# Attention, FFN and experts on one core: smaller first FFN chunks, the first in plain float32, the weights divided during the second

## The chip, the cores and the metric

One NeuronCore of a Trainium2 chip runs the whole program. The metric is device time in microseconds of one execution, as the median of several runs. PE is TensorE, DVE is VectorE, ACT is ScalarE, POOL is GpSimd and SP is SyncE, which here only issues transfers. Every engine works through its own instructions strictly in the order in which they were written out.

## The reference

```python
# attention, 4 batches x 8 heads, 576 positions, 64 wide: only the 32 largest scores of a row count
scores = q @ k.T / sqrt(64)
kth = np.partition(scores, -32, axis=-1)[..., -32:-31]
attn = softmax(np.where(scores >= kth, scores, -1e9))
x = (attn @ v)                      # laid out as 2304 tokens x 512
# dense FFN
h = np.maximum(x @ w_in, 0.0)       # 512 x 2048, weights given in 64-bit floats
x = h * h @ w_out                   # 2048 x 512
# mixture of 8 experts, two for each token, chosen by noisy logits
logits = x @ w_gate + log1p(exp(x @ w_noise)) * noise
out[token] = sum over its two experts of weight * (relu(x @ w1[e]) @ w2[e])
```

## The kernel before

**Attention** runs as 80 *units*, one after another. A full unit is 128 queries of two heads: two score tiles of 128 x 576, and for each of them a *search* on DVE for the 32nd largest value of every row (lines L407 to L448, which end in one instruction of L448 for each search). A left unit holds the last 64 queries of two heads in one score tile, so it has one search. POOL and ACT then make the softmax (L464 to L466), PE transposes it (L477, L500, L501) and multiplies it by the values (L514), and DVE scales the result (L486 or L490), which closes the unit. ACT and POOL split it into a rounded part and a remainder (`finish`, L491, L492), which go into the tile `xT` of a chunk of tokens. There are 18 token tiles of 128; `LEFT_AFTER` says after which full tile of a batch its left units come.

**The FFN** takes *chunks* of token tiles; `CHUNKS` lists their sizes. Each chunk goes through `NF` = 16 steps f. A step multiplies `xT` by a weight tile `wi` (4 parts c) into `ph` (called `pf` in the profile while attention runs), squares its positive part, and multiplies that by a weight tile `wo` into one accumulator `acc` for each token tile. Every product is made of three float32r matmuls: high by high, high by low, low by high. *First products* below are the 12 matmuls of a step with `wi` (L319 to L321), *second products* the three matmuls for each token tile with `wo` (L305 to L307). The weights arrive as 64-bit floats. `convert` makes float32 of one of the 32 weight tiles, with two instructions each on ACT (L153, L157) and DVE (L155, L156) and one on POOL (L158), divides it in high and low on ACT and POOL (L161, L162) and stores both in DRAM (`wsc`, L163), from where each chunk loads them (L313, L315). The high half of the number is worked on in PSUM (tile `acc`) for the first `IN_PSUM` = 14 conversions and in SBUF (tile `ca`) afterwards.

**What sets the order.** The FFN steps lie in a list `background`. Between the pieces of a unit, `step(n)` takes pieces of FFN work from that list up to a credit of `n` us; the credit of a unit comes from `rate(i)`. A chunk enters the list when the last unit that feeds it has closed. Three conversions are emitted for each unit at a lower priority. A scheduler with a model of the engines then fixes every engine's order. After the last unit the rest of the FFN, the routing of the last tokens (`route`) and the experts follow. These lines carry it:

```python
CHUNKS = [3, 3, 3, 3, 3, 3]
RATE = 6.0
FIRST_RATE = 5.5
def rate(i):
    return (FIRST_RATE if state["chunk"] == 0 else RATE) * (weight[i] if i < NU else 1.0)
```

Of the kernel before, what the change touches and what calls it, by code (L numbers as in the profile page):

```python
# [8 lines left out]
F32 = mybir.dt.float32  # L9
# [8 lines left out]
P = 128  # L18
# [3 lines left out]
NEG = -3.0e38  # L22
CHUNKS = [3, 3, 3, 3, 3, 3]
LEFT_AFTER = [3, 2, 0, 2]
AHEAD = 2
# [3 lines left out]
IN_PSUM = 14  # L29
RATE = 6.0  # L30
FIRST_RATE = 5.5
LEFT_WEIGHT = 0.6
# [23 lines left out]
def attention_ffn_moe(ctx: ExitStack, tc: tile.TileContext, q, k, v, w_ffn, w_route, noise, w_exp, out,  # L56
# [23 lines left out]

    tag = "" if keep is not None else "x"
    wsc = [nc.dram_tensor(f"wsc{tag}{f}", (P, 2, 2, DM), F32, kind="Internal").ap() for f in range(NF)]
    xs = nc.dram_tensor(f"xs{tag}", (E * NT, ROW), F32, kind="Internal").ap()
# [60 lines left out]
    def convert(vpool, f, which):  # L144
        n = DM
        raw = vpool.tile([P, 2 * n], U32, name="raw", bufs=3 if keep is not None else 2)
        nc.sync.dma_start(raw, w_ffn[f, which])
        pair = raw.rearrange("p (j t) -> p j t", t=2)
        lo_w, hi_w = pair[:, :, 0], pair[:, :, 1]
        a = vpool.tile([P, n], U32, name="ca", bufs=2)  # L150

# [6 lines left out]
        nc.gpsimd.tensor_tensor(a, a, lo_w, op=ALU.add)  # L158
        val = a.bitcast(F32)
        sp = vpool.tile([P, 2, n], F32R, name="csp", bufs=2 if keep is not None else 1)  # L160
# [135 lines left out]
    after, mpools = [], []  # L296

    def ffn(t0, nt, xT):
# [12 lines left out]
        for f in range(NF):  # L311
            wi = fpool.tile([P, 2, DM], F32R, name="wi", bufs=2)
            nc.sync.dma_start(wi.bitcast(F32), wsc[f][:, 0])  # L313
            wo = fpool.tile([P, 2, DM], F32R, name="wo", bufs=2)
            nc.sync.dma_start(wo.bitcast(F32), wsc[f][:, 1])  # L315
            ph = after[0].tile([P, DM], F32, name="ph") if after else ps_f.tile([P, DM], F32, name="pf")
            for c in range(NC):
                sl = slice(c * P, (c + 1) * P)
                nc.tensor.matmul(ph[:, 0:n], wi[:, 0, sl], xT[:, 0, c, 0:n], start=(c == 0), stop=False)  # L319
# [7 lines left out]
            nc.scalar.activation(r[:, 0:n], r[:, 0:n], AF.Square)  # L327
            nc.scalar.activation(gt[:, 0, 0:n], r[:, 0:n], AF.Copy)  # L328
            nc.gpsimd.tensor_tensor(gt[:, 1, 0:n], r[:, 0:n], gt[:, 0, 0:n].bitcast(F32), op=ALU.subtract)  # L329
            yield True, 0.163 * nt  # L330
# [150 lines left out]

    def finish(av, rt, dst, j, off, n):
        x = apool.tile([P, P], F32, name="x", bufs=4)
# [192 lines left out]

    def pieces(nt):
        return NF * (NC * nt * 0.163 + nt * 0.65)

# [38 lines left out]
    vctx = ExitStack()  # L718
    vpool = vctx.enter_context(tc.tile_pool(name="vpool", bufs=2))

    def conversions():
# [8 lines left out]
    for b in range(B):  # L730
        for i in range(NFULL):
            for j in range(H // 2):
                units.append((b, i * P, True, j, tiles.index((b, i))))
                if i == LEFT_AFTER[b]:
                    units.append((b, NFULL * P, False, j, tiles.index((b - b % 2, None))))
    NU = len(units)
    chunks, t = [], 0
# [25 lines left out]
    def close(i):  # L763
# [4 lines left out]
        if full:  # L768
            if ch not in dsts:
                dsts[ch] = fpool.tile([P, 2, NC, CH], F32R, name="xT", bufs=2)  # L770
            finish(av, rt, dsts[ch], j, (t - t0) * P, P)
        else:
            if t not in lefts:
                lefts[t] = apool.tile([P, 2, NC, P], F32R, name="xL", bufs=1)
            finish(av, rt, lefts[t], j, (b % 2) * LEFT, LEFT)
        missing[ch] -= 1
        if not missing[ch]:
            for tt in range(t0, t0 + nt):
                if tt in lefts:
                    nc.gpsimd.tensor_copy(dsts[ch][:, :, :, (tt - t0) * P:(tt - t0 + 1) * P], lefts[tt])  # L780
            background.append([ffn(t0, nt, dsts[ch]), pieces(nt)])

    def rate(i):

        return (FIRST_RATE if state["chunk"] == 0 else RATE) * (weight[i] if i < NU else 1.0)

# [282 lines left out]
```

## Time and profile before

| | |
|---|---|
| Median of 3 runs | 1365.13 us (1363.53 to 1368.26) |
| Profiled execution | 1361.43 us, of which 1359.7 us are the span from first to last instruction |
| PE busy | 1240.0 us, 91% |
| DVE busy | 889.0 us, 65% |
| ACT busy | 862.3 us, 63% |
| POOL busy | 773.3 us, 57% |
| Mean granted TensorE clock | 0.971 of full speed |
| Moved by DMA | 261.65 MB |

A busy share is a mean over stretches that differ: attention with FFN work between its pieces up to 781 us of the span, then what is left of the FFN, and the experts from about 895 us on.

### The profile page before, as it was taken

The page shows a single profiled execution, that of the slowest core. Times are in us where ns is not written, and L with a number is a line of the kernel's source. Part 1 is how long each engine was busy: PE and PEld are TensorE (multiplying, and loading weights), DVE is VectorE, ACT ScalarE, POOL GpSimd, SP SyncE. Part 2 cuts the span into 40 slices and gives each one's busy share as a digit, 9 for nine tenths or more (in the row PEclk, how much of TensorE's full clock was granted, in tenths as well). Part 3 has the DMA queues.
Part 4 walks back from the last instruction along what each step waited for, and adds up shares of the span by engine and source line. Part 5 has one row for each costly group of instructions (what it writes and reads, how often), then busy time and mean ns, then how long its engine had stood idle before and what let it go on. Part 6 is the DMA issues. An engine that isn't in the chain of part 4 may idle for free.

```text
span 1359.7 us, 25767 instructions
## 1 busy us (share of the span) xinstructions
PE 1240.0 (91%) x7937; PEld 1083.3 (80%) x7937; DVE 889.0 (65%) x4531; ACT 862.3 (63%) x1849; POOL 773.3 (57%) x1239
## 2 busy tenths in 40 slices
PE   3666689889999999899999998999999999999997
PEld 2554478778887888688878887889999899899876
DVE  7999979898777888998698101255544444444554
ACT  6988888898788878988797443543433323333343
POOL 5869999867875757777656536233441331513232
PEclk9787699999999999999999999999999999999999
DMA  9996688734764356166415768645653443434464
GB/s 321 362 359 232 207 298 303 257 122 136 253 215 163 122 178 226 44 198 220 153 57 176 234 245 272 221 147 194 202 165 122 134 148 124 150 114 146 137 202 139
DMA packets 86387, 261.65 MB, mean 192 GB/s; under 512 B 10844, under 2 KB 10972, under 8 KB 86240
## 3 DMA queue, kind: packets, MB, share of 16 engines
q1 hardware_dynamic: 76960, 231.51, 51.6%
q0 software_dynamic: 9280, 28.40, 5.7%
q8 instruction: 65, 1.06, 0.3%
q14 instruction: 82, 0.67, 0.2%
HBM read 209.90 MB, written 52.06 MB: 193 GB/s over the span
## 4 chain that ended last, share of the span: by engine, by line
PE 67%; DVE 9%; DMA 7%; ACT 4%; POOL 3%; issue 2%; SPq 0%; POOLq 0%; DVEq 0%; ACTq 0%
PE ph L643 5%; PE ph L644 5%; PE ph L645 5%; PE acc L624 5%; PE acc L626 5%; PE acc L625 5%; PE pa L514 4%; PE acc L305 4%; PE acc L306 4%; PE acc L307 4%; PE ps L394 4%; PE pf L319 4%; PE pf L321 3%; PE pf L320 3%; PE pa L477 3%; DVE w L411 2%
## 5 line engine op out<-in xcount | busy, mean ns | idle before, releaser
L407 DVE MAX8 m<-sb 128x8 f32<-128x115 f32 (+1 forms) x720 | 190.4, 265 | 69.5 <-ACT sb L396 64.5
L465 POOL TENSOR_TENSOR sb<-sb,w 128x576 f32<-128x576 f32 x144 | 205.7, 1430 | 46.4 <-ACT w L464 44.0
L411 DVE MATCH_REPLACE8 w<-m,sb 128x115 f32<-128x115 f32 (+1 forms) x720 | 186.9, 262 | 0.0
L665 POOL DMA_INDIRECT out<-y,info x40 | 45.9, 1148 | 241.2 <-DVE y L664 223.5
L649 ACT ACTIVATE ht<-ph 128x384 fp32r<-128x384 f32 (+1 forms) x128 | 55.8, 436 | 194.5 <-PE ph L645 194.5
L394 PE MATMUL ps<-K,qt 128*128 128x288 f32 (+2 forms) x640 | 130.6, 333 | 43.5 <-ACT sb L396 22.3
L650 DVE SCALAR_TENSOR_TENSOR ht<-ph,ht 128x384 fp32r<-128x384 f32 (+1 forms) x128 | 62.6, 489 | 162.3 <-ACT ht L649 162.2
L643 PE MATMUL ph<-xe,wi 128*128 128x256 f32 (+1 forms) x512 | 159.4, 311 | 1.7 <-ACT wi L636 1.2
L645 PE MATMUL ph<-xe,wi 128*128 128x256 f32 (+1 forms) x512 | 158.6, 310 | 0.2 <-DVE wi L637 0.2
L644 PE MATMUL ph<-xe,wi 128*128 128x256 f32 (+1 forms) x512 | 158.7, 310 | 0.0
L394 PEld LDWEIGHTS ps<-K,qt 128*128 128x128 f32 x640 | 103.4, 204 | 59.8 <-ACT sb L396 31.7
L329 POOL TENSOR_TENSOR gt<-r,gt 128x384 fp32r<-128x384 f32 x96 | 98.1, 1023 | 73.5 <-ACT gt L328 60.1
L466 ACT ACTIVATE sb<-sb,keep 128x576 f32<-128x576 f32 x144 | 112.2, 779 | 27.9 <-POOL sb L465 27.0
L624 PE MATMUL acc<-wo,ht 128*128 128x512 f32 x320 | 125.9, 397 | 0.7 <-DVE y L664 0.7
L625 PE MATMUL acc<-wo,ht 128*128 128x512 f32 x320 | 125.2, 395 | 0.0
L319 PE MATMUL pf<-xT,wi 128*128 128x384 f32 x320 | 111.9, 350 | 10.2 <-ACT xT L491 4.7
L305 PE MATMUL acc<-wo,gt 128*128 128x512 f32 x288 | 113.7, 409 | 6.3 <-DMA wo<-wsc 5.1
L464 ACT ACTIVATE w<-sb,keep 128x576 f32<-128x576 f32 x144 | 111.4, 775 | 11.7 <-POOL keep L460 11.0
L435 DVE MAX8 m<-w 128x8 f32<-128x288 f32 x288 | 115.7, 442 | 0.1
L477 PE MATMUL pa<-ident,sb 128*128 128x128 f32 x576 | 96.8, 293 | 19.1 <-ACT sb L466 10.3
L320 PE MATMUL pf<-xT,wi 128*128 128x384 f32 x320 | 110.7, 346 | 3.5 <-POOL xT L492 3.4
L306 PE MATMUL acc<-wo,gt 128*128 128x512 f32 x288 | 111.8, 402 | 0.0
(203 smaller groups left out, 3440.5 us busy)
## 6 DMA issues: line engine op xcount, KB each, us to landing
wi<-wsc SPq DMA_DIRECT2D x96, 512.0 KB, 4.7
wo<-wsc SPq DMA_DIRECT2D x96, 512.0 KB, 4.8
raww<-in_exp SPq DMA_DIRECT2D x88, 512.0 KB, 3.7
raw<-in_ffn SPq DMA_DIRECT2D x32, 512.0 KB, 6.0
wsc<-csp SPq DMA_DIRECT2D x32, 512.0 KB, 4.5
xs<-xr SPq DMA_DIRECT2D x40, 258.0 KB, 7.2
mr<-xs SPq DMA_DIRECT2D x40, 258.0 KB, 3.1
qn<-in_q SPq DMA_DIRECT2D x40, 256.0 KB, 4.2
```

Source lines behind the costliest of these rows:

```text
L305: nc.tensor.matmul(acc[tt], gt[:, 0, sl], wo[:, 0, :], start=(f == 0), stop=False)
L306: nc.tensor.matmul(acc[tt], gt[:, 0, sl], wo[:, 1, :], start=False, stop=False)
L319: nc.tensor.matmul(ph[:, 0:n], wi[:, 0, sl], xT[:, 0, c, 0:n], start=(c == 0), stop=False)
L394: nc.tensor.matmul(ps[:, n, 0:w], st, kt[:, at:at + w], start=(i == 0), stop=(i == len(pairs) - 1))
L407: in_turn(nc.vector.max(parts[i][1], sb[:, parts[i][0]]))
L411: in_turn(nc.vector.match_replace(out=w[:, sl], in_to_replace=top, in_values=sb[:, sl], imm_value=NEG))
L465: nc.gpsimd.tensor_tensor(sb, sb, w, op=ALU.subtract)
L624: queued(nc.tensor.matmul(acc[t], hs[i][:, 0, sl], wo[:, 0, :], start=(f == 0), stop=False))
L625: queued(nc.tensor.matmul(acc[t], hs[i][:, 0, sl], wo[:, 1, :], start=False, stop=False))
L643: queued(nc.tensor.matmul(ph[:, 0:n], wi[:, 0, sl], xe[i][:, 0, c, :], start=(c == 0), stop=False))
L644: queued(nc.tensor.matmul(ph[:, 0:n], wi[:, 0, sl], xe[i][:, 1, c, :], start=False, stop=False))
L645: queued(nc.tensor.matmul(ph[:, 0:n], wi[:, 1, sl], xe[i][:, 0, c, :], start=False, stop=(c == NC - 1)))
```

## The change

The chunks become 2, 2, 2, 3, 3, 3 and 3 tiles. For the first chunk `finish` writes the attention result straight into `xT`, the products are single plain float32 matmuls, and `convert` ends with the float32 weight, which it stores in a new DRAM tensor `whole`. The second chunk loads `whole`, divides it (ACT for the high part, POOL for the low part of `wi`, DVE for that of `wo`), uses the parts and stores them in `wsc`; the chunks from the third on load `wsc` as before. The credit of a unit is now the estimated work of the chunk, spread over the units that remain until the next chunk is there. The left units of batch 0 come after all its full units. The buffers `raw` and `ca` have four copies in place of three and two.

```diff
-CHUNKS = [3, 3, 3, 3, 3, 3]
-LEFT_AFTER = [3, 2, 0, 2]
+CHUNKS = [2, 2, 2, 3, 3, 3, 3]
+LEFT_AFTER = [4, 2, 0, 2]
-RATE = 6.0
-FIRST_RATE = 5.5
...
+    whole = [nc.dram_tensor(f"whole{tag}{f}", (P, 2, DM), F32, kind="Internal").ap() for f in range(NF)]
...
-        raw = vpool.tile([P, 2 * n], U32, name="raw", bufs=3 if keep is not None else 2)
+        raw = vpool.tile([P, 2 * n], U32, name="raw", bufs=4 if keep is not None else 2)
-        a = vpool.tile([P, n], U32, name="ca", bufs=2)
+        a = vpool.tile([P, n], U32, name="ca", bufs=4 if keep is not None else 2)
-        nc.scalar.activation(sp[:, 0, :], val, AF.Copy)
-        nc.gpsimd.tensor_tensor(sp[:, 1, :], val, sp[:, 0, :].bitcast(F32), op=ALU.subtract)
-        nc.sync.dma_start(wsc[f][:, which], sp.bitcast(F32))
+        nc.sync.dma_start(whole[f][:, which], a.bitcast(F32))
...
+        plain, divide = t0 == 0, t0 == CHUNKS[0]
+                if plain:
+                    nc.tensor.matmul(acc[tt], gt[:, 0, sl].bitcast(F32), wo[:, 0, :].bitcast(F32),
+                                     start=(f == 0), stop=(f == NF - 1))
+                    yield True, 0.8
+                    continue
...
+            if plain:
+                for i, w in enumerate((wi, wo)):
+                    nc.sync.dma_start(w[:, 0, :].bitcast(F32), whole[f][:, i])
+            elif divide:
+                raw = vpools[0].tile([P, 2 * DM], U32, name="raw", bufs=4 if keep is not None else 2).bitcast(F32)
+                nc.sync.dma_start(raw, whole[f].rearrange("p a d -> p (a d)"))
+                for i, (w, eng) in enumerate(((wi, nc.gpsimd), (wo, nc.vector))):
+                    part = raw[:, i * DM:(i + 1) * DM]
+                    nc.scalar.activation(w[:, 0, :], part, AF.Copy)
+                    eng.tensor_tensor(w[:, 1, :], part, w[:, 0, :].bitcast(F32), op=ALU.subtract)
+                    nc.sync.dma_start(wsc[f][:, i], w.bitcast(F32))
...
+                if plain:
+                    nc.tensor.matmul(ph[:, 0:n], wi[:, 0, sl].bitcast(F32), xT[:, 0, c, 0:n].bitcast(F32),
+                                     start=(c == 0), stop=(c == NC - 1))
...
+            if plain:
+                nc.scalar.activation(gt[:, 0, 0:n].bitcast(F32), r[:, 0:n], AF.Square)
...
+    for i, (t0, nt) in enumerate(chunks):
+        until = done_at[i + 1] if i + 1 < len(chunks) else NU
+        rates.append(pieces(nt, i == 0) / sum(weight[done_at[i] + 1:until] + [1.0]))
-        return (FIRST_RATE if state["chunk"] == 0 else RATE) * (weight[i] if i < NU else 1.0)
+        return rates[state["chunk"]] * weight[i]
```

PE in unit 10 (units are counted from 0), from the end of one value product to the end of the next, in the kernel before. L477, L500 and L501 are transposes, L394 the scores of a later unit, L514 the value product:

```order
L477 MATMUL pa<-ident,sb 128x128 x8
L319 MATMUL pf<-xT,wi 128x384
L500 MATMUL pa<-ident,sb 128x128
L501 MATMUL pa<-ident,rb 128x128
L320 MATMUL pf<-xT,wi 128x384
L321 MATMUL pf<-xT,wi 128x384
L394 MATMUL ps<-K_120,qt 128x288 x4
L514 MATMUL pa<-t_1928,vt 64x128 x2
L514 MATMUL pa<-pt,vt 64x128 x8
```

The same unit on PE after the change, without its last value product. L335 and L304 are the plain first and second products of chunk 0, L418 the scores:

```order
L501 MATMUL pa<-ident,sb 128x128 x4
L335 MATMUL pf<-xT,wi 128x256 x4
L418 MATMUL ps<-K_258,qt 128x288 x4
L501 MATMUL pa<-ident,sb 128x128 x4
L304 MATMUL acc<-wo,gt 128x512 x2
L528 MATMUL pa<-ident,sb 128x128
L335 MATMUL pf<-xT,wi 128x256 x4
L529 MATMUL pa<-ident,rb 128x128
L304 MATMUL acc<-wo,gt 128x512 x2
L418 MATMUL ps<-K_258,qt 128x288 x4
L335 MATMUL pf<-xT,wi 128x256 x4
L542 MATMUL pa<-t_1934,vt 64x128 x2
```

Three steps of the first chunk now stand in a unit in which only three matmuls of its first step stood; in the whole program the first chunk's products stand in units 5 to 16 instead of 9 to 24.

DVE in the same unit before, at its start (L411, L407, L443 and L446 belong to searches, L155 and L156 to conversions):

```order
L438 TENSOR_SCALAR low<-m 128x5x11
L411 MATCH_REPLACE w<-m,sb 128x116
L472 RECIPROCAL sm<-sm 128x2
L443 MAX low_1747<-low 128x8
L407 MAX m<-sb 128x8
L155 TENSOR_SCALAR acc<-acc 128x512
L446 MATCH_REPLACE low<-low_1747,low 128x5x11
L411 MATCH_REPLACE w<-m,sb 128x115
L156 SCALAR_TENSOR_TENSOR ca<-raw,acc 128x512
```

DVE there after the change (L154 and L155 belong to conversions, L431 to L472 to searches):

```order
L154 TENSOR_SCALAR ca<-ca 128x512
L435 MATCH_REPLACE w<-m,sb 128x115
L431 MAX m<-sb 128x8
L155 SCALAR_TENSOR_TENSOR ca<-raw,ca 128x512
L459 MAX m<-w 128x8 x2
L431 MAX m<-sb 128x8
L154 TENSOR_SCALAR ca<-ca 128x512
L462 TENSOR_SCALAR low<-m 128x5x11
L435 MATCH_REPLACE w<-m,sb 128x116
L155 SCALAR_TENSOR_TENSOR ca<-raw,ca 128x512
```

The conversions stand closer together: at the close of unit 13 all 32 are behind DVE, where 20 were; the 32nd used to stand before the close of unit 22. The tile they work on is the one in SBUF (`ca`) where it was the one in PSUM (`acc`).

SP's queue while the first chunk is under way, after the change (L158 stores a converted tile, L146 loads a raw one, L319 loads a weight tile of the first chunk):

```order
L158 DMA whole<-ca 128x512
L146 DMA raw<-in_ffn 128x1024
L319 DMA wo<-whole 128x512
L158 DMA whole<-ca 128x512
L146 DMA raw<-in_ffn 128x1024
L319 DMA wi<-whole 128x512
L319 DMA wo<-whole 128x512
```

In the kernel before a piece with loads of its first chunk (L147 raw loads, L163 stores, L313 loads for PE) reads:

```order
L147 DMA raw<-in_ffn 128x1024 x2
L163 DMA wsc<-csp 128x1024
L313 DMA wi<-wsc 128x1024
L163 DMA wsc<-csp 128x1024
L313 DMA wi<-wsc 128x1024
L147 DMA raw<-in_ffn 128x1024
L163 DMA wsc<-csp 128x1024
```

A raw load now stands behind nearly every store, and loads for PE come between them one by one; a store and a load for PE have half the bytes.

## Rows read from the trace of the kernel before

**Rows 1.** Windows of the trace by stretch: length, busy time and instruction count by engine.
```profile
core 0: us, PE busy (x) PEld busy (x) DVE busy (x) ACT busy (x) POOL busy (x), PEclk, DMA share, GB/s
0.00:154.00 154.00, 86.20 (x505) 66.14 (x505) 143.09 (x825) 123.77 (x247) 122.10 (x153) 0.81 0.87 305
154.00:193.00 39.00, 35.55 (x241) 30.91 (x242) 36.93 (x189) 35.68 (x80) 37.59 (x44) 0.96 0.78 257
193.00:262.00 69.00, 61.16 (x402) 52.29 (x401) 57.59 (x297) 58.08 (x128) 63.44 (x70) 0.98 0.85 298
262.00:314.00 52.00, 45.01 (x363) 37.47 (x361) 51.21 (x348) 46.39 (x111) 39.31 (x59) 0.97 0.37 125
314.00:414.00 100.00, 99.81 (x697) 88.63 (x697) 72.36 (x491) 80.74 (x181) 76.83 (x111) 1.00 0.64 212
457.00:538.00 81.00, 81.00 (x569) 71.77 (x567) 65.65 (x455) 68.07 (x149) 58.96 (x98) 1.00 0.59 196
538.00:578.00 40.00, 32.89 (x271) 27.31 (x268) 37.40 (x259) 37.73 (x85) 27.88 (x45) 0.96 0.19 59
676.00:700.00 24.00, 22.20 (x197) 17.74 (x196) 20.56 (x142) 20.68 (x51) 12.54 (x24) 1.00 0.10 34
700.00:781.00 81.00, 79.23 (x549) 69.92 (x549) 48.14 (x299) 55.99 (x126) 48.79 (x86) 1.00 0.56 188
781.00:895.00 114.00, 106.41 (x570) 92.71 (x570) 18.12 (x60) 51.49 (x101) 44.62 (x111) 0.99 0.68 227
```

**Rows 2.** Windows of one line alone: first L448, then L156.
```profile
0.00:154.00 154.00, 3.92 (x28) 0.81 0.87 305
538.00:578.00 40.00, 1.30 (x9) 0.96 0.19 59
...
0.00:154.00 154.00, 15.34 (x17) 0.81 0.87 305
```

**Rows 3.** Groups by line and shape: count, busy us, mean ns, then idle before.
```profile
L155 DVE TENSOR_SCALAR acc<-acc 128x512 uint32<-128x512 uint32 x14 | 9.6, 688 | 0.0
L156 DVE SCALAR_TENSOR_TENSOR ca<-raw,acc 128x512 uint32<-128x512 uint32 x14 | 9.4, 673 | 0.0
L155 DVE TENSOR_SCALAR ca<-ca 128x512 uint32<-128x512 uint32 x18 | 16.4, 909 | 6.9 <-ACT ca L153 6.9
L156 DVE SCALAR_TENSOR_TENSOR ca<-raw,ca 128x512 uint32<-128x512 uint32 x18 | 22.3, 1241 | 0.2
L637 DVE TENSOR_TENSOR wi<-raww,wi 128x512 fp32r<-128x512 f32 x88 | 61.0, 694 | 31.3 <-ACT wi L636 27.1 <-PE acc L626 0.5
L162 POOL TENSOR_TENSOR csp<-ca,csp 128x512 fp32r<-128x512 f32 x32 | 42.2, 1321 | 2.9 <-ACT csp L161 2.6 <-POOL keep L460 0.3
```

**Rows 4.** Timeline of PE: start, length, line, shape, count; the distance of starts counts.
```profile
169.73 0.40 PE L305 MATMUL acc<-wo,gt 128*128 128x512 f32 x1
169.96 0.39 PE L306 MATMUL acc<-wo,gt 128*128 128x512 f32 x1
...
427.53 1.05 PE L188 MATMUL pf<-xt,wg 128*16 128x128 f32 x8
428.51 1.57 PE L394 MATMUL ps<-K,qt 128*128 128x512 f32 x8
...
1002.12 0.34 PE L643 MATMUL ph<-xe,wi 128*128 128x384 f32 x1
1003.18 0.34 PE L643 MATMUL ph<-xe,wi 128*128 128x384 f32 x1
1004.18 0.28 PE L643 MATMUL ph<-xe,wi 128*128 128x256 f32 x1
1005.24 0.28 PE L643 MATMUL ph<-xe,wi 128*128 128x256 f32 x1
```

**Rows 5.** Waits: SP queue (total, times, longest); before tile ca (total, times).
```profile
SPq L313 <- PE pf L321: 207.2, 66, 22.9
...
  ACT ca L153: 6.9, 5
```

More of the change, by code (lines that the diff above doesn't have):

```diff
@@ L296, in attention_ffn_moe @@
     after, mpools = [], []
+    vpools = []
     def ffn(t0, nt, xT):
@@ L312, in ffn @@
             wi = fpool.tile([P, 2, DM], F32R, name="wi", bufs=2)
-            nc.sync.dma_start(wi.bitcast(F32), wsc[f][:, 0])
             wo = fpool.tile([P, 2, DM], F32R, name="wo", bufs=2)
-            nc.sync.dma_start(wo.bitcast(F32), wsc[f][:, 1])
+            if plain:
[9 more added lines that the diff above has]
+                    nc.sync.dma_start(wsc[f][:, i], w.bitcast(F32))
+            else:
+                nc.sync.dma_start(wi.bitcast(F32), wsc[f][:, 0])
+                nc.sync.dma_start(wo.bitcast(F32), wsc[f][:, 1])
             ph = after[0].tile([P, DM], F32, name="ph") if after else ps_f.tile([P, DM], F32, name="pf")
@@ L318, in ffn @@
                 sl = slice(c * P, (c + 1) * P)
+                if plain:
+                    nc.tensor.matmul(ph[:, 0:n], wi[:, 0, sl].bitcast(F32), xT[:, 0, c, 0:n].bitcast(F32),
+                                     start=(c == 0), stop=(c == NC - 1))
+                    if c < NC - 1:
+                        yield False, 0.2 * nt
+                    continue
                 nc.tensor.matmul(ph[:, 0:n], wi[:, 0, sl], xT[:, 0, c, 0:n], start=(c == 0), stop=False)
@@ L326, in ffn @@
             gt = fpool.tile([P, 2, CH], F32R, name="gt")
-            nc.scalar.activation(r[:, 0:n], r[:, 0:n], AF.Square)
-            nc.scalar.activation(gt[:, 0, 0:n], r[:, 0:n], AF.Copy)
-            nc.gpsimd.tensor_tensor(gt[:, 1, 0:n], r[:, 0:n], gt[:, 0, 0:n].bitcast(F32), op=ALU.subtract)
+            if plain:
+                nc.scalar.activation(gt[:, 0, 0:n].bitcast(F32), r[:, 0:n], AF.Square)
+            else:
+                nc.scalar.activation(r[:, 0:n], r[:, 0:n], AF.Square)
+                nc.scalar.activation(gt[:, 0, 0:n], r[:, 0:n], AF.Copy)
+                nc.gpsimd.tensor_tensor(gt[:, 1, 0:n], r[:, 0:n], gt[:, 0, 0:n].bitcast(F32), op=ALU.subtract)
             yield True, 0.163 * nt
@@ L480, in transpose4, with finish @@
         return t
-    def finish(av, rt, dst, j, off, n):
+    def finish(av, rt, dst, j, off, n, plain):
+        if plain:
+            with tc.high_priority(SOON):
+                nc.vector.tensor_tensor(dst[:, 0, j, off:off + n].bitcast(F32), av[:, 0:n], rt, op=ALU.mult)
+            return
         x = apool.tile([P, P], F32, name="x", bufs=4)
@@ L675, in attention_ffn_moe, with pieces @@
     state = {"safe": True, "due": 0.0, "chunk": 0, "routed": 0}
-    def pieces(nt):
-        return NF * (NC * nt * 0.163 + nt * 0.65)
+    def pieces(nt, plain):
+        return NF * nt * (NC * (0.2 if plain else 0.163) + (0.8 if plain else 0.65))
     def step(n):
@@ L719, in attention_ffn_moe @@
     vpool = vctx.enter_context(tc.tile_pool(name="vpool", bufs=2))
+    vpools.append(vpool)
     def conversions():
@@ L735, in attention_ffn_moe @@
                     units.append((b, NFULL * P, False, j, tiles.index((b - b % 2, None))))
+        if LEFT_AFTER[b] == NFULL:
+            units += [(b, NFULL * P, False, j, tiles.index((b - b % 2, None))) for j in range(H // 2)]
     NU = len(units)
@@ L770, in close @@
                 dsts[ch] = fpool.tile([P, 2, NC, CH], F32R, name="xT", bufs=2)
-            finish(av, rt, dsts[ch], j, (t - t0) * P, P)
+            finish(av, rt, dsts[ch], j, (t - t0) * P, P, ch == 0)
         else:
@@ L774, in close @@
                 lefts[t] = apool.tile([P, 2, NC, P], F32R, name="xL", bufs=1)
-            finish(av, rt, lefts[t], j, (b % 2) * LEFT, LEFT)
+            finish(av, rt, lefts[t], j, (b % 2) * LEFT, LEFT, False)
         missing[ch] -= 1
```

5 lines of the change are left out of this document (2 added, 3 removed).

## Prediction

> **What bounds the kernel now.** I read the windows first, by stretches cut where a unit closes. Up to 154 us DVE is busy for 143.1 us while PE has 86.2 at a granted clock of 0.81 [rows 1]: DVE sets the pace with searches and conversions, and PE has no FFN work yet. From 154 to 262 us four engines are busy at once; in 193 to 262 POOL leads with 63.4 of 69, PE has 61.2, ACT 58.1, DVE 57.6 [rows 1]. After that two kinds of stretches alternate. Where FFN work fills the units, PE is full (99.8 of 100, 81.0 of 81); where a chunk is used up before the next has come, DVE is (37.4 of 40, with PE at 32.9) [rows 1]. From 781 us on PE bounds alone, with 106.4 of 114 [rows 1]. So before 781 us the question of each stretch is which engine has most to do, and after it only how much PE has left.
>
> **Prices.** In the stretch 538 to 578 DVE ends 9 searches in 40 us [rows 1, 2], 4.4 each; up to 154 us there are 28 searches and 17 conversions [rows 2], and 154 less 14 for the start and 17 conversions at 1.4 leaves 4.1. I take 4.2 for a search with all that DVE does beside it. On PE a product of 512 columns takes 0.23 (169.73 to 169.96); six gaps of 384 columns take 1.06, so 0.177 each; nine of 256 columns also 1.06, so 0.118 [rows 4]. The stretch 457 to 538 holds 8 units with 156 first and 117 second products (counted in the order): 81 - 27.6 - 26.9 leaves 3.3 for a unit's attention on PE. A plain float32 matmul shows only in the routing (L188): 8 records, 4 matmuls of 128 columns, in 0.98 us [rows 4], so two records each and 0.122 a record. Of that 0.107 is 2 columns' time at 2.4 GHz for each column; I scale that part: 0.445 for 256 columns, 0.87 for 512. The lower bound is three high-low products (0.354 and 0.69), the upper one 0.122 a record scaled in full (0.49 and 0.98). I take the first, since it differs only in size from the row.
>
> **The change part by part.**
> The *plain chunk* costs PE 16 x (4 x 0.445 + 2 x 0.87) = 56.3 us. Divided products of two tiles would cost 16 x (12 x 0.118 + 6 x 0.23) = 44.7, so 11.6 us are added. Most of it lies in units 8 to 13. There PE has 49 plain first and 22 plain second products and six units, 21.8 + 19.1 + 19.8 = 61 us, and DVE 13 searches and 20 conversions, some 87; there it costs nothing, as long as DVE is the slower one; without that cover it is 11.6 us.
>
> *Conversions* lose one ACT and one POOL instruction, L162 with 1.32 us [rows 3], 42 us in all on POOL; 21 of these come back in the second chunk, with 16 subtractions for DVE. In the trace the same subtraction takes DVE 0.69 (L637), and L156, which also reads two SBUF tiles beside a busy POOL, 1.24 [rows 3]; so 11 to 20 us, and I take 1.0 each, 16 us. DVE's own two conversion instructions remain and move forward: 15 of them come between the counts of unit 11 before (17 conversions, 28 searches at 154 us) and unit 13 after (32 and 32). Four searches are 17 us. A conversion costs DVE 1.36 with its tile in PSUM and 2.15 in SBUF [rows 3]; all 15 are in SBUF, but POOL, 122.1 of 154 busy before [rows 1], has less to do; I take 1.8, so 27 us. Unit 13 closes at 154 + 17 + 27 = 198 (190 to 206 by the two forms).
>
> *From unit 14 on* each stretch gets what its fullest engine needs (first/second products, searches from the order of the change). Units 14 to 19: PE 44, with the last third of the plain work. 20 to 27: DVE 83 for 17 searches and 12 divisions (PE 65 for 165/82). 28 to 32: PE 29 (39/20 and routing). 33 to 39: PE 59 (153/78). 40 to 43: DVE 25 (6 searches). 44 to 52: PE 86 (168/117). 53 to 62: DVE 76 (18 searches; PE 57). 63 to 71: PE 88 (156/126). 72 to 75: PE 24. 76 to 79: PE 43 (84/63). Together 557 us. The same method gives 610 for the kernel before from 154 to 781, so 627 were 2.8% more. About a third of that excess lies in 193 to 262, where POOL led; POOL is relieved, and I add 2%: 568. Attention then ends at 198 + 568 = 766 instead of 781, a gain of 15. Bounds: no surcharge and cheap conversions, 190 + 557 = 747; 6% and dear ones, 206 + 590 = 796.
>
> The *credits* spread a chunk over all units until the next one, which is meant to fill the stretches in which DVE led. The order shows how far that goes: units 53 to 62 still hold 60 first and 36 second products, against 156 and 126 in the nine after them. So there the alternation stays.
>
> *After the last unit* 60 first and 54 second products of the chunk before the last are left, where 24 and 30 were. That is 36 x 0.177 + 24 x 0.23 = 11.9 us on an engine that is full there. From there on the order is the same.
>
> DMA moves 8.4 MB more (32 tiles of 128 x 512 floats are written once more; the seven chunks read as much as the six did), in a stretch with a DMA share of 0.87 [rows 1]; I cost it at nothing, hidden behind DVE's searches, and treat its failure as a rival.
>
> **Sum.** -15 + 12 = -3 us. The profiled execution took 1361.4 us (span 1359.7 and 1.7 around it), 3.7 below the median of the runs; the difference goes onto the median: 1365.1 - 3 = **1362 us**.
>
> **Rivals.**
> *B, the relief counts in full.* If the conversions in SBUF fall to the price of those in PSUM (1.36, 15 x 0.44 = 6.6 us less) and the mixed stretches run at what the fullest engine needs (11 us less), the time is 1362 - 18 = 1344; half of it gives 1353. For it: the four engines of 193 to 262 lose POOL as the leader. Against it: DVE and ACT are only 6 us behind in the same stretch [rows 1].
> The Trainium skill bears on this ("SBUF — State Buffer", section "Who interferes with whom"): an instruction of VectorE with two inputs in SBUF reads one through a port that it shares with GpSimd, and whoever comes second waits for the whole of the other's instruction. The trace agrees, 0.673 us with one input in PSUM against 1.241 with both in SBUF. By this rule B holds for the conversions, and it speaks against the divisions on DVE, which would wait up to one POOL instruction (1.32) each, an estimate of 16 x 2.0 = 32 us in place of 16; the mixed stretch of units 20 to 27 would then take 95 instead of 83.
>
> *C, the conversions stall DVE.* In units 8 to 13 four conversions stand in a unit. SP's queue holds the raw loads between loads for PE, which wait until PE has freed a weight tile; before, such waits came to 207.2 us in 66 cases, the longest 22.9 [rows 5]. A raw tile that comes late makes ACT late, and DVE, in order, waits with the searches behind it: L155 on the SBUF tile waited 6.9 us for ACT already, in five waits [rows 3, 5], 1.4 each. If each of 15 conversions waits 1.4, 21 us are added: 1383. It decides from 0.5 us a conversion on. Against it: four copies of the raw tile instead of three.
>
> *D, PE stays at half clock.* With PE at 1.2 GHz in units 8 to 13, the 61 us there would be 122, and 122 - 87 = 35 us would show: 1397. The granted clock of 0.81 up to 154 us speaks for it, the 0.96 from 154 on, when the first chunk ran, against [rows 1].
>
> **How the numbers follow.** My case, 1354 to 1370, gets 0.48, B 0.25, C 0.24, D 0.03. A change of less than 0.3% (4.1 us) can't be told from none here. My case reaches below 1361.0 with 0.20 of its 0.48, lies within the bound with 0.25 and above it with 0.03. So faster has 0.25 + 0.20 = 0.45, the same 0.25, slower 0.27 + 0.03 = 0.30. The range leaves out the lower part of B and the upper part of C and D, about a tenth each: 1345 to 1381.
>
> **What would show it.** In the profile after: plain first products 0.445 us apart in pairs and second ones 0.87; unit 13 closing near 198 us with DVE full until then and the granted clock high from some 115 us on; L155's SBUF form nearer to 0.67 than to 1.24; stretches of a full DVE near 540 to 615 us; the last unit closing near 766, and about 126 us instead of 114 from there until the experts alone run. The prediction is wrong if DVE has gaps before 200 us that end with ACT or a DMA (C), or if attention ends before 750 us (B).

## The result and the profile after

The changed kernel takes 1374.32 us (median of 6 runs, 1371.56 to 1379.62) against 1365.37 (1363.53 to 1368.26): a ratio of 1.0062, 95% interval 1.0041 to 1.0083. It is slower by more than the 0.3% bound; the forecast was 1362 with faster as the likeliest sign. The profiled executions lie 13.7 us apart in span (1373.4 against 1359.7), more than the medians do (9.0), because the profiled one of before was 3.9 below its median and that of the change 0.8 above; sums over stretches are made against the 13.7. Every figure by stretch below comes from one profiled execution of its kernel, and the six runs of the change alone spread over 8 us, so small differences between kernels mean little.

The windows of the changed kernel, cut again where units close (13, 19, 27, 32, 39, 43, 52, 62, 71, 75, 79; the row of units 72 to 75 is left out), answer to [rows 1]:

```profile
core 0: us, PE busy (x) PEld busy (x) DVE busy (x) ACT busy (x) POOL busy (x), PEclk, DMA share, GB/s
0.00:191.00 191.00, 134.28 (x736) 99.35 (x736) 183.06 (x960) 147.98 (x303) 130.70 (x158) 0.89 0.92 318
191.00:238.00 47.00, 41.31 (x314) 31.90 (x314) 37.49 (x239) 40.99 (x99) 36.90 (x53) 1.00 0.66 228
238.00:319.00 81.00, 71.56 (x558) 61.20 (x558) 77.85 (x465) 72.79 (x175) 69.47 (x102) 1.00 0.74 263
319.00:353.00 34.00, 31.75 (x259) 26.20 (x259) 27.55 (x187) 29.81 (x76) 21.14 (x41) 0.95 0.38 134
353.00:425.00 72.00, 66.05 (x503) 55.69 (x503) 57.88 (x379) 58.92 (x141) 60.12 (x89) 1.00 0.72 246
425.00:457.00 32.00, 28.92 (x207) 23.73 (x208) 22.03 (x149) 23.61 (x58) 17.00 (x31) 0.89 0.36 130
457.00:545.00 88.00, 86.81 (x616) 76.79 (x616) 73.46 (x496) 73.23 (x163) 60.63 (x96) 1.00 0.55 185
545.00:619.00 74.00, 64.74 (x515) 53.79 (x514) 71.80 (x499) 67.01 (x154) 50.30 (x75) 0.98 0.28 92
619.00:711.00 92.00, 90.68 (x635) 80.15 (x635) 71.04 (x483) 73.40 (x171) 65.10 (x105) 1.00 0.53 178
738.00:777.00 39.00, 39.00 (x273) 34.34 (x273) 18.07 (x96) 24.61 (x59) 21.30 (x38) 1.00 0.56 192
777.00:908.00 131.00, 120.03 (x628) 105.22 (x628) 19.00 (x67) 55.82 (x109) 53.87 (x121) 0.96 0.67 231
```

The head went as the diff says: PE has 134.3 us of work before 191 and DVE is full. In 319 to 457 no engine is full: PE has 126.7 of 138, DVE 107.5. The last row is 131 us long where 114 stood. Three sums tell where the 13.7 us are. Unit 27 closes at 319.3 instead of 308.0, 11.3 later. Units 28 to 79 take 457.4 instead of 472.9, 15.5 less. From the last close to the end it is 596.7 instead of 578.8, 17.9 more.

The conversions and divisions on DVE, by line and shape (answer to [rows 3]; count, busy, mean ns, idle before):

```profile
L154 DVE TENSOR_SCALAR ca<-ca 128x512 uint32<-128x512 uint32 x18 | 17.9, 994 | 0.0
L155 DVE SCALAR_TENSOR_TENSOR ca<-raw,ca 128x512 uint32<-128x512 uint32 x18 | 16.6, 921 | 0.0
L326 DVE TENSOR_TENSOR wo<-raw,wo 128x512 fp32r<-128x512 f32 x16 | 15.8, 988 | 5.6 <-ACT wo L325 5.6
```

The plain products, in PE's timeline (start, length, line, shape, records; answers to [rows 4]):

```profile
134.07 1.89 PE L335 MATMUL pf<-xT,wi 128*128 128x256 f32 x8
136.67 1.89 PE L304 MATMUL acc<-wo,gt 128*128 128x512 f32 x4
```

Two records make a product: four of 256 columns in 1.89 us, 0.47 each with the last one's end, and two of 512, 0.94 each. From start to start the records in these rows lie 0.216 and 0.43 us apart in the trace, which makes 0.43 and 0.87 a product.

Waits of PE for weights behind the last unit (total, times, longest), first of the change, then of the kernel before, where PE works on `ph` instead of `pf` by then:

```profile
PE pf L340 <- DMA wi<-wsc: 7.0, 1, 7.0
PE ph L319 <- DMA wi<-wsc: 4.7, 3, 2.8
```

### The profile page after: what moved, and what is told of

The parts are those of the page before. It is cut to its first block, busy times and chain, and to the rows that moved or that the text cites. A ratio compares the mean times of both kernels' runs of the same rounds, so it can differ in the third digit from the quotient of the medians.

```text
span 1373.4 us, 26178 instructions
## 1 busy us (share of the span) xinstructions
PE 1256.6 (91%) x8030; PEld 1080.9 (79%) x8030; DVE 904.1 (66%) x4557; ACT 857.6 (62%) x1879; POOL 743.7 (54%) x1229
## 4 chain that ended last, share of the span: by engine, by line
PE 60%; DVE 18%; DMA 7%; ACT 7%; POOL 3%; issue 2%; another core or an unknown queue 0%; SPq 0%; POOLq 0%; DVEq 0%; ACTq 0%
PE ph L671 5%; PE ph L673 5%; PE ph L672 5%; PE acc L652 5%; PE acc L653 5%; PE acc L654 5%; DVE w L435 4%; PE pa L542 4%; PE acc L308 3%; PE acc L310 3%; PE acc L309 3%; DVE m L431 3%; PE ps L418 3%; DVE m L459 3%; PE pa L501 3%
## 5 line engine op out<-in xcount | busy, mean ns | idle before, releaser
L431 DVE MAX8 m<-sb 128x8 f32<-128x115 f32 (+1 forms) x720 | 191.2, 266 | 44.5 <-ACT sb L420 34.8
L418 PE MATMUL ps<-K,qt 128*128 128x288 f32 (+2 forms) x640 | 131.2, 334 | 31.8 <-ACT sb L420 16.9
L418 PEld LDWEIGHTS ps<-K,qt 128*128 128x128 f32 x640 | 102.9, 204 | 48.3 <-ACT sb L420 24.3
L353 POOL TENSOR_TENSOR gt<-r,gt 128x384 fp32r<-128x384 f32 (+1 forms) x96 | 89.5, 934 | 85.2 <-ACT gt L352 71.2
L652 PE MATMUL acc<-wo,ht 128*128 128x512 f32 x320 | 125.6, 396 | 0.5 <-DVE y L692 0.5
L653 PE MATMUL acc<-wo,ht 128*128 128x512 f32 x320 | 125.2, 395 | 0.0
L488 ACT ACTIVATE w<-sb,keep 128x576 f32<-128x576 f32 x144 | 111.9, 777 | 11.9 <-POOL keep L484 11.1
L501 PE MATMUL pa<-ident,sb 128*128 128x128 f32 x576 | 96.5, 292 | 24.5 <-ACT sb L490 8.1
L340 PE MATMUL pf<-xT,wi 128*128 128x384 f32 (+1 forms) x312 | 102.9, 330 | 13.9 <-DMA wi<-wsc 7.5
L654 PE MATMUL acc<-wo,ht 128*128 128x512 f32 x320 | 108.7, 400 | 0.0
L308 PE MATMUL acc<-wo,gt 128*128 128x512 f32 x256 | 103.4, 410 | 5.6 <-ACT gt L352 3.6
L503 ACT COPY pt<-pa 128x512 f32<-128x512 f32 x144 | 83.1, 579 | 34.9 <-PE pa L501 24.7
```

Source lines behind the costliest of these rows:

```text
L418: nc.tensor.matmul(ps[:, n, 0:w], st, kt[:, at:at + w], start=(i == 0), stop=(i == len(pairs) - 1))
L431: in_turn(nc.vector.max(parts[i][1], sb[:, parts[i][0]]))
L652: queued(nc.tensor.matmul(acc[t], hs[i][:, 0, sl], wo[:, 0, :], start=(f == 0), stop=False))
L653: queued(nc.tensor.matmul(acc[t], hs[i][:, 0, sl], wo[:, 1, :], start=False, stop=False))
L654: queued(nc.tensor.matmul(acc[t], hs[i][:, 1, sl], wo[:, 0, :], start=False, stop=(f == NFE - 1)))
```

## The experiments

Three theories stood at the start. Theory 1: TensorE's sum; the earlier start fills idle time, and plain products, idle time in units 28 to 39 and the rest behind the last unit give it back. Theory 2: DVE's divisions. Theory 3: two-tile chunks alone. A fourth: the credits. Each run below gives its median and the ratio to the kernel before on the same chip. Unit closes and spans are from the profiled execution. "FFN work" is counted in the order of instructions at the prediction's prices; where a count is said to be of the trace, it is of the FFN products that start in the stretch, at the same prices.

**Parts of the change.** `chunks_only` is the kernel before with

```diff
-CHUNKS = [3, 3, 3, 3, 3, 3]
-LEFT_AFTER = [3, 2, 0, 2]
+CHUNKS = [2, 2, 2, 3, 3, 3, 3]
+LEFT_AFTER = [4, 2, 0, 2]
...
```

(and the lines that put the left units behind the full ones).

> The kernel before with the chunk sizes 2, 2, 2, 3, 3, 3, 3 alone (divided conversions and constant credits as before). By the order of instructions 22 us of FFN products stand ahead of unit 13's close instead of 4.3, and 88.6 us instead of 80.1 behind the last unit. Theory 1 (TensorE's sum: an earlier start fills its idle time, and three things give that back: plain products +11.6, idle time of 7 in units 28 to 39 where two-tile chunks load whole weights, a wait of 6 at the routing of the last tiles): the start fills some 12, the idle time and the wait stay, the dear products are gone: 1361 to 1369. Theory 2 (VectorE's divisions and its conversions make the loss): neither the loss nor plain products are here: 1352 to 1358. Theory 3 (the two-tile chunks alone make the loss): 1372 to 1378.

Measured: 1421.46, ratio 1.0400 (1.0372 to 1.0428). No theory had it: theory 3 came nearest, and by 43 us too little. Two windows show the loss:

```profile
154.00:314.00 160.00, 110.78 (x794) 90.27 (x794) 139.73 (x770) 126.42 (x287) 132.27 (x158) 0.87 0.65 219
520.00:600.00 80.00, 80.00 (x511) 68.79 (x510) 47.14 (x318) 55.38 (x119) 50.15 (x60) 1.00 0.62 206
```

Before, PE was busy for 141.7 us between 154 and 314 (three rows of [rows 1]); here for 110.8. The divided conversions still run until unit 23, and a chunk of two tiles offers two thirds of the products while they do, the next one none until the last weight is there. The trace has 32 us of FFN products between 154 and 314, where the kernel before has 68. Part of the missing work stands in units 49 to 54 (520 to 600 us), where PE is full and DVE has 47 of 80.

`rates_only` is the kernel before with the credits of the change:

```diff
-        return (FIRST_RATE if state["chunk"] == 0 else RATE) * (weight[i] if i < NU else 1.0)
+        return rates[state["chunk"]] * weight[i]
...
```

> The kernel before with the computed credits alone. By the order 87.9 us of FFN products instead of 80.1 stand behind the last unit, and as much less among the units. Theory 1: what leaves the units is paid behind them, and the wait there for weights grows by up to 6: 1365 to 1371. Theories 2 and 3: credits cost nothing, 1363 to 1367. A fourth, that the credits make the loss (TensorE, full among the units, is emptied behind them): 1372 to 1376.

Measured: 1371.67, ratio 1.0038 (1.0020 to 1.0056). The credits alone lose. The number lies between theory 1 (up to 1371) and the fourth (from 1372), so it doesn't decide between them.

`plain_only` is the change with chunks of three tiles and the old credits:

```diff
-CHUNKS = [2, 2, 2, 3, 3, 3, 3]
-LEFT_AFTER = [4, 2, 0, 2]
+CHUNKS = [3, 3, 3, 3, 3, 3]
+LEFT_AFTER = [3, 2, 0, 2]
...
-        return rates[state["chunk"]] * weight[i]
+        return (5.5 if state["chunk"] == 0 else 6.0) * weight[i]
```

> The changed kernel with chunks of 3 tiles and the constant credits of before: plain first chunk and division by the second chunk alone. The first chunk's products cost 84.4 us instead of 67.1 by the measured spacing (+17), and 23.8 us of them stand ahead of unit 13's close. Theory 1: the earlier conversions fill some 12 of idle time, 17 are paid, no idle time of two-tile chunks and no new wait at the end: 1366 to 1374. Theory 2: the divisions are all there, 1374 to 1380. Theory 3: without two-tile chunks the rest is a gain, 1350 to 1358.

Measured: 1405.55, ratio 1.0285 (1.0259 to 1.0312), above every expectation. Its windows from 200 us on:

```profile
200.00:279.00 79.00, 79.00 (x377) 47.80 (x376) 43.58 (x282) 48.26 (x103) 33.09 (x47) 1.00 0.35 113
279.00:328.00 49.00, 37.23 (x337) 29.38 (x335) 48.92 (x340) 41.40 (x99) 28.96 (x43) 1.00 0.24 81
```

The dear chunk is pressed into units 14 to 19, where PE is full and DVE has 44 of 79; then the next three tiles aren't there yet, and DVE is full while PE has 37 of 49. So early conversions need small chunks and small chunks need early conversions: small chunks alone lose 55 us, the early conversions with the plain chunk alone 39, both together, with the old credits, 4. That they need each other is measured; that it is for the reasons read from these windows is argued.

`old_credits` is the change with the constant credits:

```diff
-        return rates[state["chunk"]] * weight[i]
+        return (5.5 if state["chunk"] == 0 else 6.0) * weight[i]
```

> The changed kernel with the constant credits 5.5 and 6.0 instead of the computed ones. By the order 88.6 us of FFN products instead of 92.1 stand behind the last unit. Theory 1: the sum of TensorE's work is the same, the last close later by what the tail is shorter: 1371 to 1376. Theories 2 and 3: 1373 to 1376. The fourth (the credits make the loss): 1362 to 1367.

Measured: 1370.48, ratio 1.0028 (1.0007 to 1.0048), between the expectations. With `rates_only` it makes a square: the credits cost 0.38% on the kernel before and 0.34% on the rest of the change (1.0062 against 1.0028), about 5 us each time. The second figure is barely clear of noise, since the two intervals overlap (1.0041 to 1.0083 and 1.0007 to 1.0048).

**Terms of the sum.** `cheap_first` takes the plain price away:

```diff
-                    nc.tensor.matmul(acc[tt], gt[:, 0, sl].bitcast(F32), wo[:, 0, :].bitcast(F32),
-                                     start=(f == 0), stop=(f == NF - 1))
+                    for i in range(3):
+                        nc.tensor.matmul(acc[tt], gt[:, 0, sl], wo[:, 0, :],
+                                         start=(f == 0 and i == 0), stop=(f == NF - 1 and i == 2))
```

(and the first product in the same way, with operands rounded for it).

> The changed kernel with each plain float32 product of the first chunk replaced by three float32r products of the same operands, so that TensorE pays 44.7 us for the chunk instead of the plain price (the chunk's sums come out three times and rounded: this part of the computation is changed); everything else stands. As predicted before the run of the change (the plain price of +11.6 hidden behind VectorE in units 8 to 13): 1372 to 1376. Theory 1, that the price is paid in TensorE's sum because what it displaces comes later: 1360 to 1366.

Measured: 1363.75, ratio 1.0000 (0.9984 to 1.0017), so 0.6% below the change: theory 1's number. The gain isn't made where the products stand: unit 13 closes 4.1 us earlier, unit 27 4.5, unit 79 11.4. Another 6.8 come in units 28 to 43, which hold the same FFN products in both kernels (326 in the trace) and none of the plain ones.

`fast_credits` raises the credits behind the first chunk:

```diff
-        return rates[state["chunk"]] * weight[i]
+        return (1.25 if state["chunk"] else 1.0) * rates[state["chunk"]] * weight[i]
```

> The changed kernel with the computed credits of all chunks but the first raised by a quarter: 83.7 us of FFN products stand behind the last unit instead of 92.1, and 350.8 instead of 342.4 among the units. If TensorE's sum alone counts, nothing is won: 1371 to 1376. If products behind the last unit cost more than among the units (61 more of them took 17.5 us in the changed kernel, against 12 by their own price), 1366 to 1371. If the computed credits were well placed and the raised ones crowd TensorE in the middle, 1376 to 1385.

Measured: 1365.18, ratio 1.0016 (0.9999 to 1.0033), just below the second expectation. Unit 79 closes at 776.9, as in the change, though the order has 8.4 us more FFN work ahead of it, and from there to the last FFN product it is 95.7 us instead of 116.1. The windows of these two stretches, of `fast_credits`:

```profile
777.00:873.00 96.00, 90.92 (x476) 78.40 (x474) 7.95 (x33) 40.05 (x82) 42.29 (x91) 1.00 0.76 257
```

and of the change:

```profile
777.00:893.00 116.00, 105.83 (x544) 93.10 (x544) 13.25 (x45) 46.39 (x92) 51.17 (x109) 0.96 0.72 250
```

Of these 20.4 us 8.5 come back: from the last FFN product to the end it takes 489.1 us in `fast_credits` and 480.6 in the change, so the rest behind the last unit is 11.9 shorter (584.8 against 596.7). PE's work on the experts, of which the change had some done before its last FFN product, stands behind it now (PE is busy for 475.2 us there instead of 469.3).

`div_pool` moves the divisions of `wo`:

```diff
-                for i, (w, eng) in enumerate(((wi, nc.gpsimd), (wo, nc.vector))):
+                for i, (w, eng) in enumerate(((wi, nc.gpsimd), (wo, nc.gpsimd))):
```

> The changed kernel with both subtractions of a division on GpSimd, none on VectorE (VectorE gets some 16 us back in units 14 to 27, GpSimd gets 16 subtractions more). Theory 2 (VectorE's divisions make the loss): 1360 to 1366. Theory 1 (TensorE's sum; VectorE has room in those units): 1372 to 1377. If GpSimd becomes what the second chunk waits for: 1378 to 1390.

Measured: 1370.29, ratio 1.0048 (1.0032 to 1.0065), overlapping the change's own interval, between theory 2 (up to 1366) and theory 1 (from 1372). DVE did get its time back, and unit 27 closes 9.8 us earlier; by unit 32 the lead is 2.0 us and by unit 79 1.8. Part of the lead wasn't DVE's: 36 FFN products, 6 us by their price, that started ahead of unit 27's close in the change start behind it here. Theory 2 falls: without the divisions on DVE most of the loss is still there.

`half_loads` and its control on the kernel before, `half_loads_before`, load half of each stored weight, and the high part stands in the products for the low one:

```diff
-                nc.sync.dma_start(wi.bitcast(F32), wsc[f][:, 0])
-                nc.sync.dma_start(wo.bitcast(F32), wsc[f][:, 1])
+                nc.sync.dma_start(wi[:, 0, :].bitcast(F32), wsc[f][:, 0, 0])
+                nc.sync.dma_start(wo[:, 0, :].bitcast(F32), wsc[f][:, 1, 0])
```

> The changed kernel with only the high parts of the stored weights loaded from the third chunk on (0.5 MB a step instead of 1), the high part standing in the products where the low part stood (these products are changed, their number and sizes are not). If waits for weight loads cost what the trace shows (some 7 us of TensorE's idle time in units 28 to 39, 8 behind the last unit): 1358 to 1364. If those waits only took the place of others: 1371 to 1376.

> The kernel before with only the high parts of the stored weights loaded, in all chunks, the high part standing in the products where the low part stood (these products are changed, their number and sizes are not): the control for the same edit in the changed kernel, which gave 12. If the wait for weight loads is a loss of the change (two-tile chunks load a whole step for two thirds of the products): 1361 to 1366. If the kernel before pays it just as much: 1350 to 1356.

Measured: 1361.81, ratio 0.9990 (0.9974 to 1.0005), and 1355.94, ratio 0.9943 (0.9920 to 0.9965). Against their own kernels that is 0.7% and 0.6%. Loads cost both kernels alike, and the part of theory 1 that gave them to the change falls; without the control it would have passed for shown. Behind the last unit the halved loads show in both. From the last close to the last FFN product the change's version takes 106.2 us, where two other runs with the same 440 products there take 110.2 (`div_pool`) and 111.5 (`cheap_first`); that of before takes 95.6 with 407 products, where the kernel before takes 98.6 with 389.

**Combinations.** `fast_cheap` joins `fast_credits` and `cheap_first`, `fast_pool` joins `fast_credits` and `div_pool`, `fast15` has 1.5 in place of 1.25.

> The changed kernel with both edits that each gave some 9 to 10: three float32r products in place of each plain one in the first chunk (this part of the computation is changed) and the credits of the later chunks raised by a quarter. If the plain price and the products behind the last unit are two losses: 1353 to 1358. If both fill the same idle time of TensorE: 1361 to 1366.

> The changed kernel with the credits of the later chunks raised by a quarter and both subtractions of a division on GpSimd. The division on GpSimd alone gave 4, the credits alone 9. If both hold: 1359 to 1363, below the kernel before. If the 4 came from the shorter rest behind the last unit (440 products instead of 450) that the credits take as well: 1364 to 1367.

> The changed kernel with the credits of the later chunks raised by half: 75.9 us of FFN products behind the last unit, where a quarter left 83.7 and the changed kernel 92.1. If each product there costs more than among the units, as between the first two: 1357 to 1362. If the attention stretch has no more room for them: 1364 to 1372.

Measured: 1363.92, ratio 1.0010 (0.9993 to 1.0027); 1370.07, ratio 1.0062 (1.0039 to 1.0085); 1373.17, ratio 1.0077 (1.0053 to 1.0101). Nothing adds up: the plain price, worth 0.6% under the change's credits, is worth nothing under the raised ones. `fast_pool` and `fast15` lie above all their expectations. In `fast15` the rest behind the last unit shrinks as expected (573.8 us to the end, where the kernel before has 578.8), but unit 79 closes at 800.5, 23.6 later than in `fast_credits`.

**Attention nearly alone.** `thin_ffn` is the change, `thin_before` the kernel before (with `CHUNKS[0]` in place of the sum), with

```diff
-        for f in range(NF):
+        steps = NF if t0 < sum(CHUNKS[:2]) else 1
+        for f in range(steps):
```

> The changed kernel with one step instead of all in every FFN chunk from the third on (most of the FFN is left out), so that the attention of units 28 to 79 stands nearly alone. If the units' own chain sets units 28 to 43 (137.8 us there in the changed kernel, for 58 us of FFN products): still 125 or more there, and 1170 to 1185 in all. If the attention alone needs what VectorE is busy there (107 us) and the FFN's placement made the rest: 105 to 112 there, and 1145 to 1165 in all.

> The kernel before with one step instead of all in every FFN chunk from the second on (most of the FFN is left out): the control for the same edit in the changed kernel. If the attention's own need is the same in both, units 28 to 79 take as long as there, within 8 us, though the left units of the first batch stand elsewhere; units 20 to 27 gain from the weights being ready: 1120 to 1160 in all. If the new place of the left units makes units 28 to 43 longer: they are 10 or more shorter here.

Measured: 1259.21, ratio 0.9201 (0.9177 to 0.9225), and 1259.82, ratio 0.9214 (0.9191 to 0.9237). The totals are 74 to 100 above the expectations; behind the last unit, where little more than the experts is left, both take 533 us. The stretches are what counts. Units 28 to 43 take 126.5 us in `thin_ffn`, as its first expectation had it, and units 44 to 79 282.0:

```profile
318.00:444.00 126.00, 97.52 (x711) 76.73 (x712) 107.24 (x725) 101.59 (x233) 91.21 (x165) 0.82 0.26 86
444.00:726.00 282.00, 199.81 (x1458) 158.83 (x1456) 253.76 (x1746) 211.01 (x484) 181.73 (x321) 0.78 0.10 35
```

The same two stretches of `thin_before`:

```profile
314.00:450.00 136.00, 96.50 (x699) 74.60 (x699) 112.84 (x751) 98.30 (x229) 96.86 (x173) 0.82 0.25 81
450.00:726.00 276.00, 196.34 (x1478) 154.60 (x1477) 254.62 (x1745) 212.92 (x488) 181.15 (x321) 0.82 0.11 37
```

Both close their last unit at the same time, 726.1 and 726.3, and units 28 to 79 differ by 4.1 (408.5 and 412.6), so the left units' new place makes nothing longer. In units 28 to 43 neither is full on any engine (in `thin_ffn` DVE 107 of 126, PE 98): engines wait for each other, and PE's longest total in that stretch is for ACT, which takes the scores out of its tile:

```profile
PE ps L419 <- ACT sb L421: 12.7, 10, 3.4
```

**A shorter end.** `end_312` is `fast_credits` with

```diff
-CHUNKS = [2, 2, 2, 3, 3, 3, 3]
+CHUNKS = [2, 2, 2, 3, 3, 3, 1, 2]
```

> The changed kernel with the later credits raised by a quarter and the last three tiles of the FFN as chunks of 1 and 2: 68.9 us of FFN products behind the last unit instead of 83.7 with the raised credits alone (which gave 1365), 16 us more among the units, and 16 MB more of weights loaded. If each product behind the last unit costs 0.28 us, as eleven kernels so far show, and the last units have room: 1350 to 1360, below the kernel before. If the last units have none: 1362 to 1372.

Measured: 1453.44, ratio 1.0629 (1.0606 to 1.0652), 81 us above the highest expectation. All 32 steps of the last two chunks lie behind the last unit and take 133.3 us:

```profile
798.00:932.00 134.00, 118.15 (x595) 99.15 (x591) 7.78 (x43) 45.32 (x121) 37.64 (x89) 0.77 0.80 264
```

That is 4.2 us a step, for 2.8 us of two-tile work and 1.4 of one-tile work, with DMA at a share of 0.80 and PE's granted clock at 0.77. Taken apart, the first products of one step start 3.9 us behind those of the step before on the average, for one tile as for two. Each step loads its whole weights again. Then PE waits for the experts' rows:

```profile
PE acc L618 <- DMA mr<-xs: 20.2, 5, 12.2
```

## Why the prediction was wrong

The measured 1374 lies inside the range that it gave, 1345 to 1381, but it is a loss, to which it gave 0.30. Its sum was -15 + 12 = -3; the profile gives -4.2 + 17.9 = +13.7. In three pieces, forecast and measured: up to unit 27, +19 (198 + (44 + 83) x 1.02 = 327.5 against 308) and +11.3; units 28 to 79, -34 (430 x 1.02 = 438.6 against 472.9) and -15.5; behind the last unit +11.9 and +17.9.

**The step that failed** is "from unit 14 on each stretch gets what its fullest engine needs", and it failed in units 28 to 43. Its figures, without the 2%, and the measured ones:

| units | sum of the fullest engines | the change | `thin_ffn` |
|---|---|---|---|
| 14 to 27 | 127 | 128.2 | |
| 28 to 43 | 113 | 137.8 | 126.5 |
| 44 to 79 | 317 | 319.6 | 282.0 |

Outside units 28 to 43 the step came out within 3 us; there it is 25 us short, the most of it in units 33 to 39 (59 forecast, 71.5 measured, with PE busy for 66). What the runs show in its place: with hardly any FFN work these units already take 126.5 us, and no engine is full (DVE 107.2 of 126, PE 97.5). The lower granted clock of that run, 0.82, is not the reason: `fast_cheap` closes the same units in 126.1 us at a granted clock of 0.99, with 45 us of FFN products among them in the trace, and no kernel here does it in less (`thin_before`, in another order, takes 136.5). So 13 of the missing 25 us are attention whose engines wait for each other, which a sum of the fullest engines can't see. The other 11 (137.8 against 126.5) go with the FFN work and its place in the order: `fast_credits`, with 45 us of it there instead of the change's 53, takes 128.1, and `cheap_first`, with the same 53, 131.2. Which detail of the order does it stays open.

The forecast saving rested on these units, -27 of the -34 (115 against 142.8 in the kernel before; measured -5.0). It came from taking FFN work out of the units at its full price on PE: in the trace units 28 to 79 hold 221.9 us of it, where the kernel before has 257.5; the 36 us of difference went partly ahead of unit 28, partly behind the last unit. Units 28 to 79 came out only 15.5 us shorter. The thin pair shows what such work costs there on the average: in the change 207.5 us of FFN work (237.7 less the 30.2 left in) make units 28 to 79 longer by 48.9 us, in the kernel before 239.1 by 60.3, so a quarter of the price. Most of it goes into PE's gaps: with the attention nearly alone PE is busy for 97.5 of 126 and 199.8 of 282 us. At the lower clock of the thin pair the attention's own products take longer, so the true share may be larger than a quarter. And it is no price of a single us: 10 us more in `fast_credits` than in the change (trace) made these units 1.0 longer, 8 us more in `fast15` than in `fast_credits` 24.8.

**The second term** was the rest behind the last unit, mis-sized: 61 products more (450 against 389 in the trace) cost not 11.9 but 17.9. The profiles of ten variants bear on that price too (times in us):

| kernel | unit 27 closes | unit 79 closes | FFN products behind it | from there to the end |
|---|---|---|---|---|
| before | 308.0 | 780.9 | 389 | 578.8 |
| after | 319.3 | 776.7 | 450 | 596.7 |
| chunks_only | 313.0 | 830.5 | 431 | 588.6 |
| rates_only | 311.5 | 783.4 | 414 | 590.3 |
| plain_only | 327.9 | 822.5 | 389 | 580.9 |
| old_credits | 320.0 | 781.4 | 431 | 591.6 |
| cheap_first | 314.8 | 765.3 | 440 | 596.6 |
| fast_credits | 318.5 | 776.9 | 407 | 584.8 |
| div_pool | 309.5 | 774.9 | 440 | 592.1 |
| fast_cheap | 313.9 | 775.1 | 407 | 586.6 |
| fast_pool | 313.9 | 783.0 | 407 | 583.9 |
| fast15 | 317.3 | 800.5 | 368 | 573.8 |

From 368 to 450 products it rises by 22.9 us, 0.28 each, where the prediction had 11.9 / 61 = 0.195. Between before and after nearly all of the 17.9 lies ahead of the last FFN product (98.6 and 116.1 us from the close to it). Part of the surplus can be read: loads of `wi` held PE for 7.0 us in one wait where the kernel before has 4.7 in three, and the granted clock is 0.96 where it has 0.98. The rest of the surplus isn't explained. The line holds for steps of three tiles alone; in `end_312` a step takes 3.9 us whether it has one tile or two, which points to its load as the pace.

**The credits** were judged rightly in their place (units 53 to 62 still leave PE at 64.7 of 74) but given no time beyond the 11.9 us. The square of `rates_only` and `old_credits` makes them 0.34 to 0.38%, about half of the change's 0.62%, with the doubt of the overlapping intervals. Raising them by a quarter takes most of the loss away, raising them by half brings it back among the units.

**The plain chunk's** 11.6 us were called hidden behind DVE. DVE was indeed full (183.1 of 191), yet the products' removal moved unit 13 by 4.1 us, and the median by 0.6% under one set of credits and by nothing under another. How much of the 11.6 is paid stays open between these; it depends on what the order does with PE's later gaps.

**Right** were the prices of single instructions: plain products at 0.43 and 0.87 from start to start (forecast 0.445 and 0.87), a division on DVE 0.988 (forecast 1.0), a conversion in SBUF 0.994 + 0.921 = 1.92 (1.8), L155 in SBUF 0.92, somewhat nearer to 0.67 than to 1.24. The 2.0 us that the prediction had estimated for a division from the Trainium skill's rule ("SBUF — State Buffer", section "Who interferes with whom"), with a whole POOL instruction of waiting each time, is not borne out as an average: the 16 took 0.67 to 1.78, mean 0.99. DMA moved the 8.4 MB more (270.1 against 261.7), and the trace names no wait of DVE for a DMA in the first 200 us. Unit 13 closed at 191.1, below 198, and that was luck in the forecast's favour: its conversions were dearer than assumed (1.92 for 1.8), and the searches cheaper, 3.9 us instead of 4.2 by the same subtraction (191 less 14 for the start, 14 conversions at 1.35 and 18 at 1.92, over 32 searches). The 7 us hide part of what units 28 to 43 lost. Three slips in the recorded working change little: 13 searches at 4.2 and 20 conversions at 1.8 are 91 and not 87, the two forms give 191 to 203 for unit 13 and not 190 to 206, and in the kernel before PE had started nine FFN products by 154 us, not none. Rival C fails: DVE was busy for 183.1 of the first 191 us, and its longest wait in the first 200 was 2.0, for ACT. Rival D fails: the granted clock from 115 to 191 us, where the plain products stand, is 0.98, not a half. Rival B fails: a conversion took 1.92 and not 1.36, and attention ended at 776.7, not below 750.

**What stays open.** Variants whose order differs in details lie between 1364 and 1374 us and don't add. The additional copies of `raw` and `ca` were not tried alone. Which detail of the order makes 1365 out of 1374 beyond the credits and the rest behind the last unit was not settled. None of the versions that compute the whole beats the kernel before.

## What to carry to other kernels

The busiest engine of a stretch need not be its duration: run the stretch with the filler work taken out, and see whether the sum of the fullest engines reaches even that. Price the filler by the difference; here it was a quarter of what the engine's time said on the average, and single us of it cost between nearly nothing and three times their price, by where the order put them. Work left behind the last stretch that could hide it cost more than its own price here (0.28 us a product for 0.195); count it first, and read from the order where new credits put it. Two parts of a change that feed each other (chunk size, and how soon the weights are ready) can each be a large loss alone, so measure the pair, and run the control on the old kernel before calling a saved wait a loss of the change.

## What was not expected of the hardware

In `end_312` an FFN step behind the last unit took 3.9 us with one tile and with two, at 264 GB/s and a granted clock of 0.77. Leaving 200 us of products out of the attention shortened it by only 49 us, and PE's granted clock there fell from between 0.89 and 1.00 to about 0.8. Units 28 to 43 took 126 us with 6 us of FFN products among them (`thin_ffn`, granted clock 0.82) and with 45 (`fast_cheap`, 0.99).
